# Loading and squaring q of two couples one couple sooner, w_in's loads on POOL's queue, and a one-column PSUM write on VectorE, in an attention and feed-forward kernel

## The chip, the cores and the metric

The kernel runs on one core of one Trainium2 chip. The metric is device time in microseconds, taken as the median of several runs. A core has five engines that are used here: PE (TensorE, the matrix engine, with its weight loads shown as PEld), DVE (VectorE), ACT (ScalarE), POOL (GpSimd) and SP (SyncE, which here only issues DMAs). Each engine works through its own queue in order, and engines wait for one another through semaphores.

## What is computed

The reference is an attention block with normalised queries and keys, followed by a feed-forward block:

```python
def rmsnorm(x, g):
    rms = np.sqrt(np.mean(x * x, axis=-1, keepdims=True) + 1e-06)
    return x / rms * g
q_n, k_n = rmsnorm(q, g_q), rmsnorm(k, g_k)
scores = matmul(q_n, k_n.T) / sqrt(head_dim)
attn = exp(scores - max); attn = attn / (sum(attn) + 1e-09)
x = matmul(attn, v)                     # then (B,H,S,D) -> (B*S, H*D)
h = x @ w_in
g = h * (1.0 / (1.0 + np.exp(-h)))
out = g @ w_out
```

q, k and v have the shape (8, 12, 448, 64): 8 batches, 12 heads, 448 positions, 64 values each. x has the shape (3584, 768), w_in (768, 2048), w_out (2048, 768). All data is float32 at the reference; w_in and w_out come to the kernel as 64-bit floats, read as words of 64 bits.

## The kernel before

The kernel works in two stages in one program. The first does attention and, woven into it, the first matrix product of the feed-forward block; its results go to a DRAM tensor `hidden`. The second stage, from about 760 us on, multiplies `hidden` by w_out. The change touches the first stage only.

The work of attention is cut into 24 couples, `c` = 0 to 23. A couple is four heads of one batch, so three couples make a batch. `GROUP` is 6 couples, two batches. Couples 0 to 5 (early) and 6 to 23 (late) are handled differently: an early couple's q and k are turned by PE (`transpose_q`, `transpose_k`), a late couple's by DVE's block transpose (`flip`). The late q is loaded as 32-row quarters (eight DMAs, `load_quarters`, L249).

For each couple the program emits `visit(c)` and then `between(c)`, and this emitted order is the order of each engine's queue: no scheduler moves anything.

`visit(c)` interleaves on PE the products of scores (`scores`, L701, followed by two exponentials on ACT, L706) with the products of weights and v (`weigh`, L738). The weighing accumulates into two PSUM banks from two row halves in turn. Between the two ways of placing halves, `turn` writes one column of the second bank (L714), so that PE's next weighing waits for the write, and the write for PE's last weighing. There are two such writes in a visit: `turn(1)` near its start, done by ACT in early visits and by DVE in late ones, and `turn(0)` past its middle, done by ACT in all visits before the change. Between them a late visit emits on DVE: `divide` (L796), then in visits 6, 12 and 18 `sum_x` (L825 and L828; twelve operations in visit 6, eight in the others), in visits 7 and 9 four sums of w_in (`sum_w_in`, L825), and in visits 8 and 10 two roundings of w_in (L122, L125, L129). After `turn(0)` the next work emitted on DVE is `add(c, 1)` (L752).

`between(c)` prepares the next couple. It emits `sum_up` (row sums of the exponentials on PE, L772), two reciprocals on DVE (L781), `spread` (six DMAs, L787 and L789), the turning of q and k, `gain` (L653, ACT, on the turned k) and the normalisation of a later couple: `sum_squares` (one ACT square, L661, and one DVE reduce, L662, of q), `normalise(...)[2:]` (two ACT squares, L458, two DVE reduces, L459, and L483 of k, followed by POOL's power, L487), and `scale` (a matmul with the identity, L673; L674 on DVE; power and product on POOL, L677 and L680). `pair_up` changes the identity once, with four POOL copies (L686), ahead of the first `scale`.

PE's time in `between` is filled by matmuls of the feed-forward product (L870). `fill(others, prompt)` takes steps from an iterator, as many as are due, and deals the pieces of `others` among them; the first piece of `prompt` is emitted at once, a further one after each third step, and the rest at the end. Between couples 3 and 5 little filler exists (`make_ahead`, twelve steps in five fills); from couple 6 on there is much more.

w_in is loaded in 24 pieces of 512 KB. A piece is loaded (L84), opened (two ACT operations, L99 and L100), rounded (three DVE operations and POOL's add, L133) and then used. `round` ends with up to two calls of `load`, each only if the buffer it fills has been rounded. Three loads stand in the prologue; the others are emitted by `round`, and SP issues all of them. The saves of the product to `hidden` are issued by SP too (L903), after the activation (L1008). They free one of three buffers of `stage`, into which ACT copies a product (L888).

Of the kernel before, what the change touches and what calls it, by code (L numbers as in the profile page):

```python
# [17 lines left out]
I64 = mybir.dt.int64  # L18
# [45 lines left out]
class Rounder:  # L64
# [3 lines left out]
    def __init__(self, nc, pieces):  # L68
        self.nc = nc
        self.pieces = pieces  # L70
        self.loaded = self.opened = self.rounded = 0

    def load(self):

        i = self.loaded
        if i == len(self.pieces):
            return False
        dst, src, raw, low = self.pieces[i]
        if raw[0] is not None and raw[0] >= self.rounded:
            return False  # L80
        self.loaded += 1
        raw = raw[1]
        if src.dtype == I64:
            self.nc.sync.dma_start(raw.bitcast(I64), src)  # L84
        return True

    def open(self):
# [439 lines left out]
def bounded(  # L527
# [13 lines left out]
    GROUP = z.NPAIR  # L541
# [27 lines left out]
    rows_q = [place["q0"], extra[:, 0:nq]]  # L569
# [6 lines left out]
    late = [extra[:, ds(2 * z.NW * S - (i + 1) * n, n)].bitcast(I32) for i in range(2)]  # L576
# [10 lines left out]
        return own["second_q"] if c == 1 else raw_q[c % 2]  # L587

    def q_of(c):
        return rows_q[c % 2 if c < GROUP else 0]  # L590

    def load_q(c):

        if 0 < c < NC:
            loads["q"](c, raw_of(c) if c < GROUP else q_of(c))
# [15 lines left out]
    def transpose_q(c):  # L611

        t = ps.tile([P, 2, BANK], F32, name="sc", bufs=2)
        both = [t[:, i] for i in range(2)]
        if c == 0:
            both[1] = ps.tile([P, BANK], F32, name="av1")
        for i in range(2):
            for j in range(J):
                rows = q_of(c)[0:R, ts(i * J + j, 2 * D)]
                nc.tensor.transpose(both[i][:, ts(j, R)], rows, ident[0:R, 0:R])  # L620
            if c == 0:
                (nc.scalar.copy, nc.vector.tensor_copy)[i](qT[:, i], both[i][:, 0:S])
        if c > 0:
            nc.scalar.copy(qT, t[:, :, 0:S])
        if c == GROUP - 2:
            load_q(GROUP)

    def transpose_k(c):

# [11 lines left out]
    def flip(c, name):  # L641

        if name == "q":
            nc.vector.transpose(qT.rearrange("p i s -> p (i s)"), q_of(c)[:, 0 : z.NK])
            load_q(c + 1)
            return
        nc.vector.transpose(kT, place["k1"])
        if c + 1 < NC:
            loads["quarters"](c + 1)
# [7 lines left out]
    def sum_squares(c):  # L657

        if c >= NC:
            return  # L660
        nc.scalar.activation(squares, q_of(c)[:, 0 : z.NK], AF.Square)  # L661
        nc.vector.tensor_reduce(  # L662
            out=norm.rms[c % 2][:, 0:n], in_=squares.rearrange("p (n e) -> p n e", e=z.Q),
            axis=AX.X, op=ALU.add,
        )
# [45 lines left out]
    def turn(step, copy):  # L711

        if step != weighed["step"]:
            copy(banks[1][:, S : S + 1], minus_half)  # L714
# [85 lines left out]
    def normalise(c):  # L800


        def piece(name, i):
            if name == "q":
                norm.squares_q(c, raw_of(c), scratch[i], i)
                norm.root(c, name, i)
                norm.scale(c, raw_of(c), q_of(c), i, nc.gpsimd)
                if i == 1 and c + 2 < GROUP:
                    load_q(c + 2)
            else:  # L810
                late = c >= GROUP
                rows = place["k0" if late else f"k{c % 2}"]
                norm.squares_k(c, rows, scratch[0 if late else i], i)
                if i == 1:
                    norm.root(c, name)
                    if late and c + 1 < NC:
                        loads["k"](c + 1)

        if c >= NC:
            return []  # L820
        return [lambda a=a: piece(*a) for a in (("q", 0), ("q", 1), ("k", 0), ("k", 1))]
# [540 lines left out]

    def visit(c):

        if c < GROUP - 1:
            beside = normalise(c + 1)
        elif c == GROUP - 1:
            beside = [lambda: sum_squares(c + 1), lambda: scale(c + 1)] + normalise(c + 1)[2:]
        else:
            beside = []  # L1370
        if c < NC:
            scores(c, 0, 0)
        run_all(beside[0:1])
        if c > 0:
            weigh(c - 1, LEFT)
            weigh(c - 1, LEFT - 1, 0)
            turn(1, nc.scalar.copy if c < GROUP else nc.vector.tensor_copy)
        if c < NC:
            scores(c, 0, 1)
        if c == 0:  # L1380
            run_all(beside[1:2])
        if c > 0:
            weigh(c - 1, LEFT - 1, 1)
            if c - 1 < EARLY:
                for i in range(2):
                    nc.vector.tensor_copy(x_of(c - 1, i), sums[i])
                run_all(beside[1:2])
                if inverting:
                    if c > 1:
                        divide(c - 2, None)  # L1390
                    run_all(inverting)
                    inverting.clear()
            else:
                divide(c - 1, sums)
                run_all(beside[1:2])
                if c < NC and c % GROUP == 0:
                    for i in range(0 if c == GROUP else 1, HW):
                        sum_x(last_two(c), i)
                weights_in_visit(c)
            if c + 1 < NC:  # L1400
                loads["vrest"](c + 1)
        if c == NC:
            return
        scores(c, 1, 0)
        scores(c, 1, 1)
        if c < GROUP:
            run_all(beside[2:3])
        weigh(c, 0, 1)
        scores(c, 2, 0)
        weigh(c, 1, 1)  # L1410
        turn(0, nc.scalar.copy)
        if c < GROUP:
            run_all(beside[3:4])
        scores(c, 2, 1)
        weigh(c, 0, 0)
        run_all(add(c, 1))
        weigh(c, 1, 0)
        scores(c, LEFT)
        if c + 1 < NC:
            loads["v"](c + 1)  # L1420

    def run_all(work):
        for piece in work:
            piece()

    def between(c):

        def transposes_and_sums():
            summing = sum_up(c)
            if c < GROUP:  # L1430
                next(summing)
            if c < GROUP - 1:
                transpose_k(c + 1)
            reciprocals = next(summing)
            if GROUP - 1 <= c < NC - 1:
                reciprocals += [lambda: flip(c + 1, "k"), gain]
            if GROUP // 2 <= c <= EARLY:
                divide(c - 1, None)
            return reciprocals

        if c < GROUP - 1:
            transpose_q(c + 1)
        elif c < NC - 1:
            flip(c + 1, "q")
        if c < GROUP // 2:
            inverting.extend(transposes_and_sums())
        elif c == GROUP - 1:
            run_all(transposes_and_sums())
        if c >= GROUP and c % GROUP == 0:
            fetched = range(AHEAD) if c == GROUP else ()  # L1450
            columns = products - 2 * HW * S * len(fetched)
            work = halves_in(last_two(c), range(HF), plain_in, dict(begun), fetched)
            begin(work, columns, 2 * GROUP)
            begun.clear()
        late = add(c, LEFT - 1) + add(c, LEFT) if c >= GROUP else []
        further = normalise(c + 2)[2:] if c >= GROUP - 1 else []
        queries = [lambda: sum_squares(c + 2)] if c >= GROUP - 1 else []
        fill(late + weights_in(c, 0) + further)
        prompt = transposes_and_sums() if GROUP // 2 <= c != GROUP - 1 else []
        if c == GROUP // 2:  # L1460
            begin(make_ahead([0, 1]), AHEAD * 2 * HW * S, GROUP - 1)
        fill(weights_in(c, 1), prompt[:3] + [lambda: run_all(prompt[3:] + queries)])
        if c == GROUP - 2:
            pair_up()
        if c % GROUP == GROUP - 1:
            finish()
            if c == GROUP - 1:
                begun[0] = fetch_ahead([0, 1], 0)
            else:
                sum_x([c // GROUP * 2, c // GROUP * 2 + 1], 0)  # L1470
        if c >= GROUP - 1:
            scale(c + 2)
        if GROUP <= c < NC - 1:

            nc.scalar.activation(first, minus_half, AF.Exp)
        if c == NC - 1:
            while rounder.load():
                pass
# [2 lines left out]
    load_q(2)  # L1481
    for _ in range(2):
        room.w_in.load()
    transpose_k(0)
    transpose_q(0)
    for c in range(NC):
# [228 lines left out]
```

## Time and profile before

| what | value |
|---|---|
| median of 3 runs | 1344.02 us (1342.76 to 1345.15) |
| the profiled execution, its own time | 1346.0 us |
| its span, first to last instruction | 1344.1 us |
| mean granted clock of TensorE | 0.994 |
| first column write of a late visit (L714 on DVE) | 19 instances, median 0.162 us |
| column writes on ACT (L714) | 29 instances, median 0.173 us |
| w_in loads issued by SP (L84) | 24 of 512 KB, some 5 us to landing |
| DMAs issued by POOL in the whole run | 4, of 0.539 to 0.759 us on POOL each |

The profile is one execution taken by the hardware profiler. A row of its timeline has the start in microseconds from the span's start, the length, the engine (a q behind it is the sequencer that issues a DMA), the line of the program, the operation, what is written and read, the shape and a count; in square brackets stands the idle time of the engine before it and what ended that. A matmul of float32 shows as two records. A table by windows gives for each stretch its length, the busy time of PE, PEld, DVE, ACT and POOL with counts, the granted clock, the DMA share and the rate. Holes of PE are read from the brackets in PE's rows.

### The profile page before, as it was taken

The page shows a single profiled execution, that of the slowest core. Times are in us where ns is not written, and L with a number is a line of the kernel's source. Part 1 is how long each engine was busy: PE and PEld are TensorE (multiplying, and loading weights), DVE is VectorE, ACT ScalarE, POOL GpSimd, SP SyncE. Part 2 cuts the span into 40 slices and gives each one's busy share as a digit, 9 for nine tenths or more (in the row PEclk, how much of TensorE's full clock was granted, in tenths as well). Part 3 has the DMA queues.
Part 4 walks back from the last instruction along what each step waited for, and adds up shares of the span by engine and source line. Part 5 has one row for each costly group of instructions (what it writes and reads, how often), then busy time and mean ns, then how long its engine had stood idle before and what let it go on. Part 6 is the DMA issues. An engine that isn't in the chain of part 4 may idle for free.

```text
span 1344.1 us, 19812 instructions
## 1 busy us (share of the span) xinstructions
PE 1300.4 (97%) x7111; PEld 828.3 (62%) x7111; DVE 951.8 (71%) x1630; ACT 502.3 (37%) x877; POOL 369.5 (27%) x223
## 2 busy tenths in 40 slices
PE   8997998999999999999999999999999999999997
PEld 4332443444444444444444455557999999999997
DVE  5786876785855655855554586789978787878785
ACT  7874455556445545455544244420000000101000
POOL 5765344443343343343331044410000000000000
PEclk9998999999999999999999999999999999999999
DMA  8565456434433543443421257422323232332311
GB/s 230 155 147 123 119 155 161 106 89 109 108 91 88 124 93 87 124 97 86 112 74 38 101 176 262 149 98 71 103 75 99 75 102 77 99 100 79 125 48 39
DMA packets 286543, 147.69 MB, mean 110 GB/s; under 512 B 224420, under 2 KB 270372, under 8 KB 286436
## 3 DMA queue, kind: packets, MB, share of 16 engines
q1 hardware_dynamic: 285872, 145.35, 39.6%
q8 instruction: 58, 0.95, 0.3%
q0 software_dynamic: 256, 0.79, 0.2%
q14 instruction: 49, 0.40, 0.1%
q10 hardware_dynamic: 308, 0.20, 0.0%
HBM read 96.73 MB, written 41.29 MB: 103 GB/s over the span
## 4 chain that ended last, share of the span: by engine, by line
PE 81%; DVE 7%; ACT 4%; DMA 3%; issue 2%; SPq 2%; POOL 0%; ACTq 0%; DVEq 0%
PE mm L870 24%; PE alone L1177 22%; PE av L738 8%; PE sc L701 8%; PE mm L1177 7%; PE alone L870 7%; PE alone L1214 2%; DVE work L781 1%; DVE work L752 1%; DMA rows<-in_k_dram 1%; PE sc L772 1%; SPq L249 1%; DVE sums_x L825 1%; PE mm L1214 1%; ACT L1008 1%
## 5 line engine op out<-in xcount | busy, mean ns | idle before, releaser
L870 PE MATMUL mm<-x,W 128*128 128x448 f32 x636 | 258.6, 549 | 12.0 <-DVE parts L828 3.3
L706 ACT ACTIVATE work<-sc,rms 128x448 f32<-128x448 f32 x324 | 185.5, 635 | 86.2 <-PE sc L701 62.8
L870 PEld LDWEIGHTS mm<-x,W 128*128 128x128 f32 x636 | 117.6, 191 | 146.8 <-issue 114.7
L870 PE MATMUL mm<-sums_x,W 128*128 128x448 f32 x456 | 186.5, 548 | 6.8 <-DVE parts L828 4.8
L701 PE MATMUL sc<-work 64*64 64x448 f32 x1344 | 167.3, 550 | 1.7 <-DVE rms L674 1.1
L738 PE MATMUL av<-work,rows 64*64 64x448 f32 x1296 | 156.0, 546 | 4.7 <-ACT av L714 1.8
L752 DVE TENSOR_TENSOR work<-work 128x896 f32<-128x896 f32 (+1 forms) x114 | 123.7, 1115 | 49.4 <-PE av L738 48.8
L870 PEld LDWEIGHTS mm<-sums_x,W 128*128 128x128 f32 x456 | 85.1, 191 | 100.2 <-issue 83.4
L487 POOL TENSOR_TENSOR rms<-rms,minus_half 128x14 f32<-128x14 f32 (+3 forms) x37 | 88.3, 2389 | 134.6 <-DVE rms L483 133.9
L514 POOL DMA_DIRECT2D out_dram<-x x2 | 1.3, 652 | 443.0 <-DVE x L828 443.0
L1177 PE MATMUL alone<-W,rows 128*128 128x192 f32 x608 | 113.0, 326 | 0.0
L738 PEld LDWEIGHTS av<-work,rows 64*64 64x64 f32 x1296 | 60.7, 133 | 76.0 <-issue 35.4
L677 POOL TENSOR_TENSOR rms<-rms,minus_half 128x28 f32<-128x28 f32 x18 | 86.2, 4791 | 74.7 <-DVE rms L674 63.3
L1177 PEld LDWEIGHTS alone<-W,rows 128*128 128x128 f32 x608 | 101.2, 190 | 0.0
L701 PEld LDWEIGHTS sc<-work 64*64 64x64 f32 x1344 | 55.5, 134 | 69.1 <-ACT work L706 26.9
L890 POOL TENSOR_TENSOR parts<-parts,stage 128x448 f32<-128x448 f32 x31 | 42.0, 1355 | 150.3 <-DVE parts L828 149.9
L1177 PE MATMUL alone<-W,work 128*128 128x192 f32 x382 | 72.2, 326 | 0.0
L1008 ACT ACTIVATE stage<-stage 128x896 f32<-128x896 f32 x63 | 57.4, 947 | 24.7 <-DVE stage L828 24.1
L1177 PEld LDWEIGHTS alone<-W,work 128*128 128x128 f32 x382 | 63.8, 190 | 0.0
L1187 ACT COPY rows<-alone 128x192 f32<-128x192 f32 x34 | 10.9, 320 | 137.4 <-PE alone L1177 78.9
L781 DVE RECIPROCAL work<-sc 128x224 f32<-128x224 f32 x36 | 55.6, 1547 | 5.2 <-PE sc L772 5.0
L459 DVE TENSOR_REDUCE rms<-rows 128x8 f32<-128x512 f32 (+2 forms) x48 | 30.2, 629 | 40.3 <-ACT rows L458 37.5
(243 smaller groups left out, 2104.9 us busy)
## 6 DMA issues: line engine op xcount, KB each, us to landing
hidden<-stage SPq DMA_DIRECT2D x63, 448.0 KB, 3.1
work<-hidden SPq DMA_DIRECT2D x21, 1024.0 KB, 5.1
rows<-in_moe_w_out_dram SPq DMA_DIRECT2D x32, 384.0 KB, 3.4
W<-in_moe_w_in_dram SPq DMA_DIRECT2D x22, 512.0 KB, 5.0
work<-work SPq DMA_DIRECT2D x144, 56.0 KB, 2.0
rows<-in_q_dram SPq DMA_DIRECT2D x144, 56.0 KB, 2.3
rows<-in_k_dram SPq DMA_DIRECT2D x144, 56.0 KB, 2.4
x<-hidden SPq DMA_DIRECT2D x7, 1024.0 KB, 5.6
```

The costliest lines, as they stand in the source:

```text
L487: nc.gpsimd.tensor_tensor(out=t, in0=t, in1=half, op=ALU.pow)
L677: nc.gpsimd.tensor_tensor(out=f, in0=f, in1=minus_half.to_broadcast([P, n]), op=ALU.pow)
L701: nc.tensor.matmul(two[ds(half * D, D), h, 0:S], keys[rows, ts(half, D)], qT[rows, pair, :], start=True, stop=True,)
L706: nc.scalar.activation(eleft[:, h] if j == LEFT else weights(c, j)[:, i, h], two[:, h, 0:S], AF.Exp, scale=norm.column(c, i, h, j),)
L738: nc.tensor.matmul(sums[i][ds(h * D, D), :], v, w, start=(j == 0 and step == 1), stop=(j == LEFT - 1 and step == 1),)
L752: nc.vector.tensor_tensor(out=total, in0=total, in1=more, op=ALU.add)
L781: nc.vector.reciprocal(out=r[0][:, rows], in_=t[:, rows])
L870: nc.tensor.matmul(t, self.left(name, s), self.right(name, s), start=s == ends[0], stop=s == ends[1])
L890: nc.gpsimd.tensor_tensor(out=u2, in0=u2, in1=p5, op=ALU.add)
L1008: nc.scalar.activation(t, t, AF.Silu)
L1177: nc.tensor.matmul(t, x[:, i], y, start=i == ORDER[0], stop=i == ORDER[-1])
L1214: nc.tensor.matmul(o, a[:, 2 * i + m, t], right_one(name, i)[:, m], start=n == 0, stop=n == len(steps) - 1,)
```

## The change

Four things are edited together.

The q of couple 6 is squared and scaled, and its k squared, in `between(4)` and no longer in `visit(5)`. The q of couple 7 is loaded by `transpose_q(5)` in `between(4)` (before: by `flip(6, "q")` in `between(5)`), into the buffer that q of couple 5 leaves; q of couple 8 is loaded by `flip(6, "q")`, and `flip(7, "q")` loads nothing.

In `between(5)`, `transposes_and_sums` is no longer run as a whole ahead of the first fill. Its PE part still is; the two reciprocals, the spreading, the flip of k and `gain` are handed to that fill as `prompt`.

The w_in loads that `round` emits are issued by POOL.

`turn(0)` of visits 6 to 23 is a DVE copy.

```diff
@@ class Rounder
+        self.queue = nc.sync
...
-            self.nc.sync.dma_start(raw.bitcast(I64), src)
+            self.queue.dma_start(raw.bitcast(I64), src)
@@ q_of(c)
-        return rows_q[c % 2 if c < GROUP else 0]
+        return rows_q[c % 2 if c < GROUP + 2 else 0]
@@ transpose_q(c)
-        if c == GROUP - 2:
-            load_q(GROUP)
+        if c >= GROUP - 2:
+            load_q(c + 2)
@@ flip(c, name)
-            load_q(c + 1)
+            if c != GROUP + 1:
+                load_q(c + 2 if c == GROUP else c + 1)
@@ visit(c)
-        if c < GROUP - 1:
-            beside = normalise(c + 1)
-        elif c == GROUP - 1:
-            beside = [lambda: sum_squares(c + 1), lambda: scale(c + 1)] + normalise(c + 1)[2:]
-        else:
-            beside = []
+        beside = normalise(c + 1) if c < GROUP - 1 else []
...
-        turn(0, nc.scalar.copy)
+        turn(0, nc.scalar.copy if c < GROUP else nc.vector.tensor_copy)
@@ between(c)
-        elif c == GROUP - 1:
-            run_all(transposes_and_sums())
...
-        further = normalise(c + 2)[2:] if c >= GROUP - 1 else []
-        queries = [lambda: sum_squares(c + 2)] if c >= GROUP - 1 else []
-        fill(late + weights_in(c, 0) + further)
+        further = normalise(c + 2)[2:] if c >= GROUP - 2 else []
+        queries = [lambda: sum_squares(c + 2)] if c >= GROUP - 2 else []
+        prompt = transposes_and_sums() if c == GROUP - 1 else []
+        fill(late + weights_in(c, 0) + further, prompt)
...
-        if c >= GROUP - 1:
+        if c >= GROUP - 2:
             scale(c + 2)
@@ bounded, ahead of the loop over couples
     for _ in range(2):
         room.w_in.load()
+    room.w_in.queue = nc.gpsimd
```

## The prediction

> **What bounds the kernel now.** I read the page first, then PE's row of the timeline for holes, then the engine named as the releaser of each hole, in the stretches that the change touches. The page says that PE is the bound:
>
> ```profile
> span 1344.1 us, 19812 instructions
> ...
> PE 1300.4 (97%) x7111; PEld 828.3 (62%) x7111; DVE 951.8 (71%) x1630; ACT 502.3 (37%) x877; POOL 369.5 (27%) x223
> ```
>
> So an edit counts only as far as it opens or shuts a hole in PE, and 97% is an average: the holes lie in a few places. Three of them bear on this change. The first is between couple 5 and couple 6 (PE's timeline):
>
> ```profile
> 119.36 1.02 PE L870 MATMUL mm<-x,W 128*128 128x448 f32 x2
> 122.76 4.12 PE L870 MATMUL mm<-x,W 128*128 128x448 f32 x6 [2.38 <-DVE work L781]
> 130.80 0.62 PE L673 MATMUL sc<-rms,ident 128*128 128x28 f32 x2 [3.92 <-DVE rms L662]
> 131.36 1.03 PE L701 MATMUL sc<-work 64*64 64x448 f32 x4
> ```
>
> PE waits 2.38 us for the reciprocal, then 3.92 us for the reduce of `sum_squares(7)`. Only four matmuls of filler (eight records) lie in this gap, so DVE and ACT set its length. Two stretches of the table by windows show a third loss, the clock, after the hole and its twin near 232 us:
>
> ```profile
> 129.47:132.88 3.41, 2.08 (x10) 1.05 (x14) 3.15 (x6) 1.26 (x3) 2.59 (x2) 0.50 0.59 102
> 132.88:136.29 3.41, 3.41 (x24) 1.24 (x20) 0.12 (x2) 1.16 (x2) 3.41 (x2) 0.50 0.61 118
> 235.28:238.69 3.41, 3.41 (x6) 1.38 (x6) 2.39 (x3) 0.60 (x1) 2.19 (x3) 0.50 0.17 43
> ```
>
> The value after POOL's is the granted clock, 0.50. A 3.41 us stretch in which PE stood idle for 2.02 us or more is followed by one at half clock, which costs 3.41/2 = 1.7 us of matmuls.
>
> The second place is the gap after couple 8 (timelines of SP, ACT and PE):
>
> ```profile
> 203.58 1.52 SPq L249 DMA_DIRECT2D rows<-in_k_dram  x3
> 213.00 3.51 SPq L84 DMA_DIRECT2D W<-in_moe_w_in_dram  x2
> ```
> ```profile
> 226.22 0.90 SPq L903 DMA_DIRECT2D hidden<-stage  x2
> ```
> ```profile
> 229.50 0.53 ACT L888 COPY stage<-mm 128x448 f32<-128x448 f32 x1 [8.56 <-DMA hidden<-stage]
> ```
> ```profile
> 230.08 2.52 PE L870 MATMUL mm<-x,W 128*128 128x448 f32 x6 [2.55 <-ACT stage L888]
> 234.62 2.00 PE L870 MATMUL mm<-sums_x,W 128*128 128x448 f32 x3 [2.02 <-DVE parts L828]
> ```
>
> SP stands from 205.1 to 213.0 behind a w_in load that waits for POOL's add. So the saves of hidden issue at 226.2, ACT waits 8.56 us for the first to land, and PE waits 2.55 and 2.02 us and then runs one stretch at half clock.
>
> The third place is visit(6), in DVE's timeline and in the one of the moment when the one-column write runs on ACT:
>
> ```profile
> 137.90 1.16 DVE L796 TENSOR_TENSOR x<-av,work 128x448 f32<-128x448 f32 x2 [1.55 <-PE av L738]
> 138.97 1.73 DVE L825 TENSOR_TENSOR sums_x<-x 128x448 f32<-128x448 f32 x1
> ...
> 146.34 0.62 DVE L825 TENSOR_TENSOR sums_x<-x,sums_x 128x448 f32<-128x448 f32 x1
> 146.87 1.08 DVE L752 TENSOR_TENSOR work<-work 128x896 f32<-128x896 f32 x1
> ```
> ```profile
> 141.96 0.17 ACT L714 COPY av<-minus_half 128x1 f32<-128x1 f32 x1
> 142.19 0.14 PEld L738 LDWEIGHTS av<-work,rows 64*64 64x64 f32 x3 [0.35 <-ACT av L714]
> ```
>
> PE's next weighing is released by the write at 142.13, while DVE works through twelve `sum_x` operations without a pause until 146.96. L752 at 146.87 is `add(6, 1)`, the first DVE instruction that stands after the write in the emitted order.
>
> [...]drops at 2.02 us of idle within a window, but not at 1.6 us (the hole before 151.5 us). [...]the four POOL issues of this trace take 0.54 to 0.76 us each. [...](an L825 of 0.62 us takes 2.12 us beside POOL L680 at 353.95).
>
> **The write on VectorE.** `turn(0)` of couples 6 to 23 moves into DVE's in-order queue, behind `divide`, `sum_x` and `weights_in_visit`. Where DVE is idle (11 visits; DVE idles 4.44 us before L752 in visit 11) nothing is lost; PE's start follows ACT's copy by 0.05 us, so at most 11 x 0.05 = 0.5 us is gained. In seven visits DVE is behind. The write then starts where L752 starts now, takes 0.16 us (DVE's L714 median), and PE follows 0.05 us later. L752's start plus 0.21, less PE's present start: visit 6: 147.08-142.19 = 4.9; visit 7: 179.29-177.26 = 2.0; visit 8: 214.12-211.76 = 2.4; visit 9: 253.74-251.80 = 1.9; visit 10: 287.65-285.29 = 2.4; visit 12: 357.92-354.99 = 2.9; visit 18: 562.26-559.25 = 3.0. Sum 19.5 us. Queued behind the write on DVE is only `add(c, 1)`, which waits for that weighing and so starts some 1.3 us later. PE arrives later at holes that DVE sets now, which gives back: after visit 6 holes of 1.97 and 0.49; after visit 7 about 0.7 (what 2.0 exceeds DVE's 1.3); after 8 about 0.5 of 1.03; after 9 0.3; after 10 about 1.2 of 1.86 and 0.94. Together 5.2, leaving 14.3. After visits 12 and 18 no such hole follows, so their 5.9 us stay whole. Idle stretches of 2 to 5 us also trip the clock: bounds 0 and 7 x 1.7 = 12 us. [...]I take about half, 5.5.
>
> **Couple 6 squared in the gap before visit 5.** `normalise(6)` for k (two ACT squares, two DVE reduces, L483), `sum_squares(6)` and `scale(6)` leave visit(5), where PE hid them but for a hole of 0.24 and two matmuls (0.55 in all). They enter between(4), where the filler is short. DVE's rows there:
>
> ```profile
> 103.04 0.95 DVE L825 TENSOR_TENSOR W<-W 128x768 f32<-128x768 f32 x1
> 103.90 1.55 DVE L781 RECIPROCAL work<-mm 128x224 f32<-128x224 f32 x1
> 106.59 1.09 DVE L662 TENSOR_REDUCE rms<-rows 128x28 f32<-128x896 f32 x1 [1.14 <-ACT av L714]
> ```
>
> DVE ends this work at 105.45 while PE enters visit(5) at 103.36. The added reduces, 0.69+0.55+0.18 with their ping-pong with ACT, push `divide(3)` from 98.02 to 99.7, and the second reciprocal to about 106.8; L662 (1.09), now queued behind it, ends at 107.9, and the matmul of `scale(6)` stands ahead of visit(5) on PE. PE starts visit(5) at 108.25: +4.9, less 0.55. POOL's four copies of `pair_up` end near 107.3, just before. The hole of 3.4 us or so trips the clock: +1.7 (bounds 0 and 3.4).
>
> **Couple 7, one gap later.** q(7)'s eight loads now issue in between(4), but their landing (125.5) was not what L662 waited for: ACT's third square started at 128.68, on the reduce before it. The number of DVE and ACT operations in between(5) is unchanged; `run_all` becomes pieces dealt in the fill, so squares and rounding stand ahead of the second reciprocal, flip and `gain`. Counting from the end of visit(5)'s matmuls (115.64 before): adds +1.0, flip 2.1, divide 3.2, reciprocal 4.75, rounding 6.35, two reduces and L483 8.4, reciprocal 9.95, flip 11.0, `gain` 12.05, square 13.0, reduce 14.1; before, the matmul of `scale(7)` came at +15.16. So 1.0 is saved, and the slow clock ends about 1.1 us cheaper, because more of it falls into the hole. The loads of q(7), k(7), q(8) and k(8) that pass the spreading DMAs on SP delay these by some 4 us; `divide(4)` and `divide(5)` come later still, so this is hidden. This part: 4.35+1.7-1.0-1.1 = +4.0.
>
> **Loads on POOL.** 21 of the 24 w_in loads leave SP. Elsewhere SP's wait for POOL, or the 0.4 us of each issue, ended in no hole of PE. After couple 8 it did: saves would issue near 223, land near 226, and PE would not wait: -2.55-2.02-1.7 = -6.3 (bounds: 0, if the late q loads or the stage buffers hold the saves, and -6.3). POOL pays about 0.65 us for each[...]. Most lie in idle POOL; the four after couple 0 push q of couple 2 from 38.0 to 39.4, and PE wants it at 39.3. I take +0.7 in all[...].
>
> **The sum.** 14.3 + 5.5 - 0.5 + 4.0 - 6.3 + 0.7 = +17.7. Against the profiled execution that is 1346.0 (span 1344.1, 1.9 around it) to 1363.7; the median shown, 1344.0, lies 2.0 below that execution, so the forecast is 1361.7.
>
> **Rivals.** *Given back*: the DVE-bound stretches after visits 6 to 10 return all but 2.4 of those five waits and the clock never drops: 5.9+2.4-0.5+2.3-6.3+0.7 = +4.5, 1348.5. For it: five holes set by DVE follow there. Against: the clock did drop after 2.02 us.[...] *The other side*: in between(5) the reordering lets filler and reduces run beside each other, so both holes and the slow clock shut: 2.38+3.92 and about 4.2 of clock = -10.5; with -6.3 after couple 8 and waits of 14.3 without clock loss: -10.5-6.3+14.3-0.5+0.7 = -2.3, 1341.7. It decides once the waits net under some 16 us. Against: the same chain of DVE and ACT operations remains and there is no more filler. That the write isn't held by DVE's queue I exclude: L752 shows that queue in order.
>
> **Chances.** Forecast 0.73 (1351 to 1373 by its bounds), given back 0.12[...], the other side 0.07. Range 1348 to 1373: it takes in the lower rival and leaves out the other side[...]. About 0.2% (2.7 us) can be told from no change: faster 0.07, same 0.04, slower 0.89.
>
> **What would show it.** DVE L714 with 37 instances; PE holes before L738 released by DVE L714 of 2 to 5 us in visits 6 to 10, 12 and 18; a hole of 3 to 4 us before L673 ahead of visit(5); no ACT wait of 8 us for hidden<-stage after couple 8. I am wrong if those PE holes are under 1 us, or if between(5) shrinks by more than 3 us.

## The result, and the profile after

| | median, us | runs |
|---|---|---|
| before | 1343.65 (1342.76 to 1345.15) | 4 |
| after | 1363.36 (1362.46 to 1364.35) | 4 |

The ratio is 1.0146, 95% interval 1.0128 to 1.0163: slower by 19.7 us. The forecast was 1361.7. The profiled execution of after has a span of 1362.5 us (its own time 1364.35), 18.4 more than the one of before. In after the lines of the code named here stand one or two further down: the column write is L716, the weighing L740, the filler L872, the matmul of `scale` L675, the reduce of `sum_squares` L664. The page of after:

```profile
span 1362.5 us, 19838 instructions
...
PE 1305.3 (96%) x7111; PEld 826.0 (61%) x7111; DVE 951.5 (70%) x1648; ACT 500.7 (37%) x859; POOL 379.2 (28%) x244
...
L740 PE MATMUL av<-work,rows 64*64 64x448 f32 x1296 | 161.0, 564 | 21.8 <-DVE av L716 16.5
```

PE has the same 7111 records and 4.9 us more of busy time: matmuls at half clock, which are longer (below, 3.26 us for sixteen records where 1.73 is seen at full clock). The other 13.5 of the 18.4 us are idle time of PE. DVE and ACT swap eighteen instructions and POOL gains its 21 issues, and none of these engines is busier in a way that matters. The last line says where: of 21.8 us that PE stood idle ahead of the weighing, 16.5 were ended by DVE's write. The table of PE's waits in after (line that waited, releaser, us in total, times, longest) sets this beside the others:

```profile
PE av L740 <- DVE av L716: 16.5, 7, 4.3
PE sc L675 <- DVE rms L664: 10.6, 3, 6.8
PE mm L872 <- DVE parts L830: 3.7, 6, 1.7
PE av L740 <- DMA rows<-in_v_dram: 2.5, 1, 2.5
```

In the kernel before the same table has 1.5 us (once, in the last visit) in place of the 16.5, 4.7 in place of the 10.6, 8.1 in place of the 3.7 for the row of parts, and 0.9 in place of the 2.5 for v: each of the changed parts shows in this table.

**The write.** The timeline of PE in after, in visits 6, 9, 12 and 18:

```profile
145.94 1.20 PE L703 MATMUL sc<-work 64*64 64x448 f32 x8
151.40 3.26 PE L740 MATMUL av<-work,rows 64*64 64x448 f32 x16 [4.25 <-DVE av L716]
...
258.27 1.73 PE L740 MATMUL av<-work,rows 64*64 64x448 f32 x16
...
365.13 2.21 PE L740 MATMUL av<-work,rows 64*64 64x448 f32 x16 [2.56 <-DVE av L716]
...
573.84 2.70 PE L740 MATMUL av<-work,rows 64*64 64x448 f32 x16 [2.58 <-DVE av L716]
```

The other holes of this kind are 1.62 us (visit 7, at 187.05), 1.93 (visit 8, at 223.70) and 2.01 (visit 10, at 293.67). In visit 9 there is none to speak of: 0.14 us. DVE's timeline shows why PE waits in visit 6; the one-column write comes directly behind the last of twelve sums, without a pause:

```profile
150.66 0.62 DVE L827 TENSOR_TENSOR sums_x<-x,sums_x 128x448 f32<-128x448 f32 x1
151.19 0.15 DVE L716 COPY av<-minus_half 128x1 f32<-128x1 f32 x1
```

And the table by windows (length; busy us of PE, PEld, DVE, ACT, POOL; granted clock; DMA share; GB/s) shows what follows such a hole. The stretch after it runs at half clock, and the 3.26 us of the sixteen records at 151.40 compare with 1.73 for sixteen at 258.27:

```profile
147.78:151.20 3.42, 0.00 (x0) 0.00 (x0) 3.39 (x8) 0.58 (x2) 0.00 (x0) 1.00 0.05 10
151.20:154.61 3.41, 3.21 (x20) 1.21 (x24) 1.45 (x4) 0.00 (x0) 0.00 (x0) 0.50 0.00 0
```

(Matmuls begun before 147.78 end there by the model, so PE's 0.00 in the first row is the hole.)

**The gaps before visits 5 and 6.** PE and then DVE in after:

```profile
103.91 1.77 PE L872 MATMUL mm<-x,W 128*128 128x448 f32 x4 [2.23 <-DVE stage L830]
108.80 0.38 PE L675 MATMUL sc<-rms,ident 128*128 128x28 f32 x2 [3.12 <-DVE rms L664]
...
135.24 0.60 PE L675 MATMUL sc<-rms,ident 128*128 128x28 f32 x2 [6.77 <-DVE rms L664]
```
```profile
106.16 1.55 DVE L783 RECIPROCAL work<-mm 128x224 f32<-128x224 f32 x1
107.63 1.03 DVE L664 TENSOR_REDUCE rms<-rows 128x28 f32<-128x896 f32 x1
```

Before visit 5 the reduce now stands behind the second reciprocal and ends at 108.66, and PE waits for it. Before visit 6 the two holes of 2.38 and 3.92 us have become one of 6.77.

**After couple 8.** SP, ACT and PE in after:

```profile
228.00 5.40 SPq L250 DMA_DIRECT2D rows<-in_q_dram  x8
233.50 0.90 SPq L905 DMA_DIRECT2D hidden<-stage  x2
```
```profile
236.85 0.53 ACT L890 COPY stage<-mm 128x448 f32<-128x448 f32 x1 [4.15 <-DMA hidden<-stage]
```
```profile
236.98 3.27 PE L872 MATMUL mm<-x,W 128*128 128x448 f32 x8
241.97 2.52 PE L872 MATMUL mm<-sums_x,W 128*128 128x448 f32 x6 [1.72 <-DVE parts L830]
```

ACT still waits for the saves, now behind the eight loads of q and not behind w_in, but for 4.15 us in place of 8.56. The hole of 2.55 us is gone, that of 2.02 is 1.72, and no half-clock stretch follows. This can't be put down to the loads on POOL alone: e2 and e9 below shorten the same gap with all loads on SP.

**What no case of the prediction had: v of visit 2.** PE, POOL and SP in after:

```profile
51.09 0.98 PE L740 MATMUL av<-work,rows 64*64 64x448 f32 x8 [2.46 <-DMA rows<-in_v_dram]
```
```profile
42.73 1.17 POOL L85 DMA_DIRECT2D W<-in_moe_w_in_dram  x2
46.68 0.55 POOL L85 DMA_DIRECT2D W<-in_moe_w_in_dram  x1 [0.30 <-POOL W L134]
```
```profile
43.52 0.53 SPq L321 DMA_DIRECT2D rows<-in_v_dram  x1
44.10 1.68 SPq L324 DMA_DIRECT2D rows<-in_v_dram  x2
```

The first of these three loads of v lands 6.4 us after its issue (in before, where it is issued at 43.72, 3.4 us), with three pieces of w_in of 512 KB each on the way at the same time (e5 shows that these are the cause). In before, SP issued them at 49.70, behind v and k in its queue. The hole is followed by a half-clock stretch from 52.2.

The ledger of the two profiled executions, by the starts and ends of the scores of each visit:

| part | predicted, us | after less before, us |
|---|---|---|
| visits 6, 7, 8, 9, 10, 12, 18 (waits and clock) | 19.5 + 5.5 | 6.2 + 1.9 + 2.2 + 0.4 + 3.7 + 4.4 + 4.5 = 23.3 |
| gaps behind 6, 7, 9 and 10 | -4.7 | -2.8 (6), -0.2 (9), -2.5 (10) = -5.5 |
| gap before visit 5, and visit 5 | +4.35 + 1.7 | 4.5 + 0.5 = 5.0 |
| gap before visit 6 | -1.0 - 1.1 | -1.8 |
| gap after couple 8 (the write, the loads on POOL) | -0.5 - 6.3 | -5.9 |
| visits 2 to 4 (POOL's price) | +0.7 | 3.9 - 1.3 = 2.6 |
| idle visits | -0.5 | within the remainder |
| start, before visit 1 | 0 | -1.3 |
| behind visit 23 | 0 | +2.3 |

The right column sums to 18.7, the spans differ by 18.4. (The 4.4 of visit 12 has 0.4 of the gap behind it.) The -1.3 at the start is there with only the write moved too (-1.4), where nothing in that place was touched; it is scatter between executions.

### The profile page after: what moved, and what is told of

Same layout as the page of the kernel before. It is cut to its first block, busy times and chain, and to the rows that moved or that the text cites. A ratio compares the mean times of both kernels' runs of the same rounds, so it can differ in the third digit from the quotient of the medians.

```text
span 1362.5 us, 19838 instructions
## 1 busy us (share of the span) xinstructions
PE 1305.3 (96%) x7111; PEld 826.0 (61%) x7111; DVE 951.5 (70%) x1648; ACT 500.7 (37%) x859; POOL 379.2 (28%) x244
## 4 chain that ended last, share of the span: by engine, by line
PE 78%; DVE 11%; DMA 3%; ACT 3%; SPq 2%; issue 2%; POOL 0%; ACTq 0%; DVEq 0%; POOLq 0%
PE mm L872 22%; PE alone L1179 22%; PE av L740 8%; PE mm L1179 7%; PE alone L872 7%; PE sc L703 7%; PE alone L1216 2%; SPq L250 2%; DVE sums_x L827 2%; DVE work L783 1%; DMA rows<-in_k_dram 1%; PE sc L774 1%; DVE W L827 1%; DVE work L754 1%; DMA work<-work 1%
## 5 line engine op out<-in xcount | busy, mean ns | idle before, releaser
L872 PE MATMUL mm<-x,W 128*128 128x448 f32 x636 | 256.8, 547 | 6.1 <-DVE stage L830 3.1
L872 PEld LDWEIGHTS mm<-x,W 128*128 128x128 f32 x636 | 117.2, 190 | 140.4 <-issue 112.2
L872 PE MATMUL mm<-sums_x,W 128*128 128x448 f32 x456 | 184.7, 544 | 3.1 <-DVE parts L830 2.3
L740 PE MATMUL av<-work,rows 64*64 64x448 f32 x1296 | 161.0, 564 | 21.8 <-DVE av L716 16.5
L703 PE MATMUL sc<-work 64*64 64x448 f32 x1344 | 170.1, 559 | 2.2 <-DVE rms L676 1.2
L872 PEld LDWEIGHTS mm<-sums_x,W 128*128 128x128 f32 x456 | 85.1, 190 | 95.6 <-issue 85.5
L754 DVE TENSOR_TENSOR work<-work 128x896 f32<-128x896 f32 (+1 forms) x114 | 121.8, 1099 | 25.9 <-PE av L740 24.2
L740 PEld LDWEIGHTS av<-work,rows 64*64 64x64 f32 x1296 | 59.3, 136 | 98.9 <-issue 38.9
L1189 ACT COPY rows<-alone 128x192 f32<-128x192 f32 x34 | 10.8, 318 | 136.9 <-PE alone L1179 88.2
L1193 ACT COPY rows<-alone 128x192 f32<-128x192 f32 x34 | 10.8, 319 | 123.7 <-PE alone L1179 120.1
```

The costliest lines, as they stand in the source:

```text
L703: nc.tensor.matmul(two[ds(half * D, D), h, 0:S], keys[rows, ts(half, D)], qT[rows, pair, :], start=True, stop=True,)
L740: nc.tensor.matmul(sums[i][ds(h * D, D), :], v, w, start=(j == 0 and step == 1), stop=(j == LEFT - 1 and step == 1),)
L754: nc.vector.tensor_tensor(out=total, in0=total, in1=more, op=ALU.add)
L872: nc.tensor.matmul(t, self.left(name, s), self.right(name, s), start=s == ends[0], stop=s == ends[1])
```

## The experiments

All these kernels compute everything that the reference asks for. Times are medians; each ratio is to runs of the kernel before on the same chip.

**e1: all of the change but the write.** After, with

```diff
-        turn(0, nc.scalar.copy if c < GROUP else nc.vector.tensor_copy)
+        turn(0, nc.scalar.copy)
```

> The changed kernel with turn(0) of the late visits back on ACT, all else as changed. Theory (the write queued behind DVE's work in seven visits is the main cost, some 18 to 20 us with the clock it trips): 1343 to 1346 us; no hole of PE before the weighing of visits 6 to 10, 12 and 18 over 0.3 us, granted clock 1.0 from visit 8 to the end of the stage but for chance. Rival (the early squaring of couple 6 is the main cost, the write's waits are mostly given back): at least 1355 us.

Measured: 1346.53 us, ratio 1.0028 (1.0017 to 1.0038). That is half a microsecond above what was expected. By the medians the write is worth 16.8 us of the 19.7. Of the holes that DVE's write sets before a weighing, only the one of 1.5 us in the last visit is left, and before has that too.

**e2: the write alone.** Before, with the line of e1 the other way round.

> The kernel before with turn(0) of visits 6 to 23 on DVE alone. Theory: slower than before by 14 to 20 us (1358 to 1364), with holes released by DVE's write of about 4.9, 2.0, 2.4, 1.9, 2.4, 2.9 and 3.0 us less what PE's skew hides, in visits 6 to 10, 12 and 18, and none over 0.2 us in the other eleven. Rival: slower by under 8 us, since the holes set by DVE after visits 6 to 10 shrink by as much.

Measured: 1363.79 us, ratio 1.0153 (1.0139 to 1.0167), inside the expected 1358 to 1364. The holes, in PE's timeline of this kernel:

```profile
143.88 3.26 PE L738 MATMUL av<-work,rows 64*64 64x448 f32 x16 [4.87 <-DVE av L714]
...
256.38 1.73 PE L738 MATMUL av<-work,rows 64*64 64x448 f32 x16 [1.53 <-DVE av L714]
```

The first is as long as the 4.9 us that were worked out for visit 6, and visit 9 has its hole here. So the 0.14 us of visit 9 in after belongs to the other parts: there DVE gets to its write 8.7 us after the start of the visit, here after 10.1. The loads on POOL have a share in that: with them alone DVE gets to `add` in visit 9 after 9.65 us (e3 and e5), in before after 10.10. The rest isn't settled.

By the starts and ends of the scores, the seven visits are 26.5 us longer than in before, and the gaps behind visits 6 to 10 are 3.0, 0.0, 3.9, 0.4 and 2.5 us shorter, 9.7 in all. (This trace lies 1.6 us below the median of its kernel and that of before 2.1 above its own, so the spans differ by 16.3 us where the medians differ by 19.9.) After couple 8 the hole of 2.55 us is gone here too, though SP issues all loads: PE comes later.

**e3: w_in's loads on POOL alone.** Before, with

```diff
+        self.queue = nc.sync
...
-            self.nc.sync.dma_start(raw.bitcast(I64), src)
+            self.queue.dma_start(raw.bitcast(I64), src)
...
+    room.w_in.queue = nc.gpsimd
```

> The kernel before with the w_in loads that round emits issued by POOL, alone. Theory: faster than before by 4 to 6 us (1338 to 1340): the 8.6 us wait of ACT for hidden<-stage after couple 8, PE's holes of 2.55 and 2.02 us and the half clock there are gone (-6.3), and a hole of some 2 us in visit 2, where v lands late, costs 1 to 2. Rival (issues on POOL are dear for POOL and DVE): no faster than before, 1343 us or more.

Measured: 1343.88 us, ratio 1.0000 (0.9992 to 1.0008). A miss: the gap after couple 8 is 4.9 us shorter, but there is a loss around visit 2. Its hole in PE's timeline of this kernel, in which the lines stand one further down than before:

```profile
51.39 1.77 PE L739 MATMUL av<-work,rows 64*64 64x448 f32 x8 [2.68 <-DMA rows<-in_v_dram]
```

With the half-clock stretch behind it, visit 2 is 3.8 us longer; from the end of visit 1 to the end of visit 4 the loss is 2.7. Of the 4.9 us after couple 8, 2.0 show also where nothing in that place was touched (see e9), which leaves 2.9 for the loads: gain and loss about cancel.

**e5: the same loads on POOL, but only from couple 6 on.** Made after e3, to see whether the hole comes from those early issues. As e3, with the last line put inside the loop over couples, under `if c == GROUP:`.

> The kernel before with the w_in loads issued by POOL only from couple 6 on, by SP until then. Theory (issuing on POOL gains some 5 us after couple 8 and loses it in visits 1 to 4, where w_in's packets run beside those of v and k instead of behind them): the hole of 2.7 us in visit 2 is gone, the one after couple 8 stays gone, 1338 to 1340.5 us. Rival (POOL's own time for the issues is the loss, wherever they are): 1342 us or more.

Measured: 1340.88 us, ratio 0.9980 (0.9971 to 0.9988): faster than before by 2.5 us, and just above what was expected. Two views of this kernel, SP and PE:

```profile
224.08 0.90 SPq L904 DMA_DIRECT2D hidden<-stage  x2
```
```profile
47.90 1.68 PE L702 MATMUL sc<-work 64*64 64x448 f32 x16
49.57 0.98 PE L739 MATMUL av<-work,rows 64*64 64x448 f32 x8
...
232.08 2.52 PE L871 MATMUL mm<-sums_x,W 128*128 128x448 f32 x6 [1.49 <-DVE parts L829]
```

The weighing at 49.57 follows without a hole, and the saves, issued at 224.08 and not at 226.22, leave only the hole of 1.49 us behind couple 8 (that gap is 4.8 us shorter, with the same 2.0 in it). The early issues on POOL are thus what costs in visit 2; by the medians of e3 and e5 they cost 2.5 us.

**e4: the early squaring and the dealing, without the write and without POOL.** After, with the write as in e1 and without the line `room.w_in.queue = nc.gpsimd`.

> The changed kernel without the write on DVE and without the loads on POOL: only the earlier q and k of couples 6 to 8 and the pieces dealt in the gap after couple 5. Theory: slower than before by 2.5 to 5 us (1346.5 to 1349): PE waits some 3 us for DVE's reduce ahead of visit 5, then runs one stretch at half clock, and the gap after couple 5 is 1 to 2 us shorter. Rival (the early loads and squares do what they are for, and the trace of the changed kernel shows the loads on POOL in their way): faster than before by 2 us or more.

Measured: 1345.74 us, ratio 1.0020 (1.0013 to 1.0026): slower, but at 1.8 us by the medians short of the 2.5 to 5 that were expected. PE's timeline of this kernel:

```profile
102.43 3.20 PE L872 MATMUL mm<-x,W 128*128 128x448 f32 x4 [2.24 <-DVE stage L830]
107.32 0.38 PE L675 MATMUL sc<-rms,ident 128*128 128x28 f32 x2 [1.69 <-DVE rms L664]
```

Visit 5 starts 4.3 us later, near the 4.9 that was foreseen, and takes 11.12 us in place of 12.35, since the norms of couple 6 have left it. The half clock lies from 102.6 to 106.0, over the four records of filler (3.20 us, in after 1.77) whose end PE's wait follows anyway; so it costs nothing. In after it lies over visit 5, which takes 12.81 us.

**e7: the dealing alone**, with q(7) and q(8) loaded sooner and couple 6 still squared in visit 5. Before, with the change's edits of `q_of`, `transpose_q` and `flip`, and with

```diff
-        elif c == GROUP - 1:
-            run_all(transposes_and_sums())
...
-        fill(late + weights_in(c, 0) + further)
+        prompt = transposes_and_sums() if c == GROUP - 1 else []
+        fill(late + weights_in(c, 0) + further, prompt)
```

> The kernel before with the gap after couple 5 dealt as in the change (reciprocals, flip and gain as prompt pieces of the fill; q of couples 7 and 8 loaded one couple sooner), but couple 6 squared and scaled in visit 5 as before. Theory (the gap after couple 5 gains 1 to 2 us, and the early squaring ahead of visit 5 is what loses): faster than before by 1 to 3 us (1341 to 1343). Rival (the dealing is what loses): slower than before.

Measured: 1344.53 us, ratio 1.0006 (0.9997 to 1.0015): no difference to be told, and a miss. PE before visit 6, in this kernel:

```profile
122.16 2.52 PE L872 MATMUL mm<-x,W 128*128 128x448 f32 x6 [0.62 <-ACT stage L880]
131.45 0.60 PE L675 MATMUL sc<-rms,ident 128*128 128x28 f32 x2 [6.77 <-DVE rms L664]
```

The hole of 2.38 us moved into the one of 3.92; the gap is 0.5 us shorter (15.14 for 15.65), not 2. In e4 and in after it is 1.8 shorter. DVE's timeline shows why, in e7 and then in e4:

```profile
115.36 1.45 DVE L484 TENSOR_SCALAR rms<-rms 128x14 f32<-128x14 f32 x1
116.73 2.09 DVE L754 TENSOR_TENSOR x<-x,work 128x896 f32<-128x896 f32 x2
```
```profile
117.35 2.09 DVE L754 TENSOR_TENSOR x<-x,work 128x896 f32<-128x896 f32 x2 [4.48 <-PE av L740]
```

L754 opens DVE's work for this gap, and from its start to the matmul of `scale` it is 14.7 us in both (15.2 in before). In e7 it stands behind the last piece of couple 6's normalisation and starts together with PE's row sums (116.77); in e4 DVE has been idle for 4.48 us, and it starts 1.3 us ahead of them (118.67). So the dealing is worth 0.5 us, and the other 1.3 come from the norms that have left visit 5.

**e8: e7 and e5 together.**

> The dealing of the gap after couple 5 and the loads on POOL from couple 6 on, together; turn(0) on ACT, couple 6 squared in visit 5. Theory: the two gains lie in different gaps and add up, 1335 to 1338.5 us, faster than both kernels. Rival: the first gain is eaten by a later wait, and it is as the run with the late loads on POOL alone.

Measured: 1339.94 us, ratio 0.9972 (0.9961 to 0.9983): above what was expected by about as much as e7 was, and at 3.5 us under the kernel before the fastest of all kernels here; its interval overlaps that of e5, so what the dealing adds isn't shown.

**e6: the write on DVE, put ahead of DVE's sums.** Before, with

```diff
-        if c > EARLY:
-            if c < NC and c % GROUP == 0:
-                for i in range(0 if c == GROUP else 1, HW):
-                    sum_x(last_two(c), i)
-            weights_in_visit(c)
...
-        turn(0, nc.scalar.copy)
+        turn(0, nc.scalar.copy if c < GROUP else nc.vector.tensor_copy)
+        if c > EARLY:
+            if c < NC and c % GROUP == 0:
+                for i in range(0 if c == GROUP else 1, HW):
+                    sum_x(last_two(c), i)
+            weights_in_visit(c)
```

> The kernel before with turn(0) of late visits on DVE, and sum_x and the rounding and summing of w_in in visits emitted just behind that write instead of ahead of it. Theory (the place in DVE's queue is the cost, not the engine): no hole before the weighing over 0.3 us in visits 6 to 10, 12 and 18, and a time within 5 us of the kernel before (1342 to 1349), as add(c, 1) now comes later. Rival (a DVE write of PSUM releases PE later than an ACT write, or collides with other DVE work): holes of over 1 us stay and the time is over 1352.

Measured: 1355.57 us, ratio 1.0076 (1.0062 to 1.0090). Half a hit: the holes before the weighing are gone, so it was the place in the queue; but the time lies where the rival had it. DVE and PE in this kernel:

```profile
140.49 0.16 DVE L714 COPY av<-minus_half 128x1 f32<-128x1 f32 x1 [2.83 <-PE av L738]
140.56 0.62 DVE L825 TENSOR_TENSOR sums_x<-x 128x448 f32<-128x448 f32 x1
```
```profile
146.42 1.77 PE L870 MATMUL mm<-sums_x,W 128*128 128x448 f32 x4 [1.24 <-DVE sums_x L825]
...
157.31 1.02 PE L870 MATMUL mm<-sums_x,W 128*128 128x448 f32 x2 [2.22 <-DVE parts L828]
```

Now DVE stands idle for 2.83 us until PE's weighing lets it write, its sums begin that much later, and PE waits for the sums: the gaps behind visits 6, 7, 9, 10, 12 and 18 are 13.1 us longer together. Here the write costs on both sides: what is ahead of it delays it (e2), and what is behind it is delayed by what the write waits for (e6).

**e9, e10, e11: the write on DVE in some visits only.** Before, with `nc.vector.tensor_copy` in `turn(0)` for visits 12 and 18 (e9), for the eleven visits in which DVE is idle (e10), and for visits 6 to 10 (e11).

> The kernel before, with the second one-column write on VectorE in visits 12 and 18 only. Theory (the write waits in VectorE's queue, and nothing that follows these two visits gives the wait back): two PE holes of 2.5 to 3 us before the weighing, 5.9 us in all, each with one half-clock stretch of 1.7 us: 5.9 to 9.3 us over the kernel before, 1349.5 to 1353. Rival (PE's later arrival is absorbed by the next thing that VectorE or ScalarE would have held up, as after visits 6 to 10): under 1346.

> The kernel before, with that write on VectorE in visits 11, 13 to 17 and 19 to 23 only, where VectorE has nothing queued ahead of it. Theory (only the place in the queue costs, VectorE itself is not dearer than ScalarE for one column): within 1 us of the kernel before, 1342.7 to 1344.5, with no PE hole over 1 us before these weighings. Rival (the write on VectorE costs by itself in each of the eighteen visits, some 1.1 us each): about 1356.

> The kernel before, with that write on VectorE in visits 6 to 10 only. Theory (waits of some 13 us in all, of which about 5 are given back at holes that VectorE sets already, and a few half-clock stretches): what the write costs alone (about 20 us) less what visits 12 and 18 cost, so 10 to 14 us over the kernel before, 1353.5 to 1358. Rival (nearly all is given back after these visits): under 1348.

Measured: e9 1355.47 us, ratio 1.0088 (1.0074 to 1.0101); e10 1343.86, ratio 1.0002 (0.9994 to 1.0010); e11 1349.83, ratio 1.0052 (1.0039 to 1.0066). Above the kernel before, by medians, 12.3, 0.7 and 6.7 us, together 19.7, where e2 has 19.9. So the eleven writes are free, and only the place in the queue costs. But by these medians two visits out of seven make most of the price: e9 came out 2.5 us above the theory's range, e11 3.7 us below it. PE's timeline and the table by windows of e9:

```profile
356.73 2.50 PE L738 MATMUL av<-work,rows 64*64 64x448 f32 x16 [2.56 <-DVE av L714]
...
565.42 2.97 PE L738 MATMUL av<-work,rows 64*64 64x448 f32 x16 [2.58 <-DVE av L714]
```
```profile
354.35:357.76 3.41, 1.03 (x12) 0.59 (x16) 2.29 (x5) 1.03 (x2) 0.04 (x1) 0.97 0.00 0
357.76:361.18 3.42, 3.42 (x17) 0.96 (x11) 2.42 (x3) 0.38 (x1) 0.00 (x0) 0.53 0.15 35
```

In this execution (its own time is 1354.3) visit 12 is 4.3 and visit 18 is 4.5 us longer: 8.8 together, 5.9 of wait and some 3 of clock, as the theory has it, and they keep it to the end. The profiled execution of before (1346.0) is 8.3 below that. But it lies 2.9 above the median of the seventeen runs of before here, and the one of e9 1.1 below its own; so about 4 us of the 12.3 are in no trace. Where they are stays open. Differences between executions do show in places that no edit touches; in e9 the largest is the gap after couple 8, 2.0 us shorter than in before. PE's timeline of e9 there:

```profile
230.24 3.87 PE L870 MATMUL mm<-x,W 128*128 128x448 f32 x6 [2.00 <-ACT stage L888]
234.78 2.52 PE L870 MATMUL mm<-sums_x,W 128*128 128x448 f32 x6 [0.67 <-DVE parts L828]
```

Here the half-clock stretch (from 231.27) lies over the six records between the two holes, 3.87 us for 2.52 in before, and fills most of the second, 0.67 us in place of 2.02; in before it came behind both (from 235.28) and cost its full 1.7. In e10 the longest waits for the same two releasers, ACT's copy and DVE's parts, are 2.3 and 2.1 us, near the two holes of before.

What e11 has too little is in its trace: visits 6 to 10 are 15.8 us longer and the gaps behind them 9.1 shorter, not 5, which makes the 6.7 that were measured.

## Why the prediction was right, point by point

**The time.** 1361.7 was forecast and 1363.36 measured. The main term was right; that the sum came so near is partly luck. By themselves the parts measure +19.9 (the write, e2; 19.3 predicted), +1.8 (couple 6 and the dealing, e4; +4.0) and -0.1 (the loads, e3; -6.3 + 0.7 = -5.6): two errors in opposite directions, -2.2 and +5.5. The three add up to 21.6 and the change measures 19.7; the intervals of the change and of e2, about 2 us either way, don't tell the two sums apart.

**The write on VectorE: right in mechanism and, as a sum, in size.** Its terms were 14.3 + 5.5 - 0.5 = 19.3 us; alone it measures 19.9 (e2), with the others in place 16.8 (after less e1). The rule used, that PE starts where L752 started plus 0.21 us, is borne out: against the start of its visit PE's weighing comes later in e2 than in before by 2.03, 2.36, 1.93, 2.35, 2.94 and 3.01 us in visits 7 to 10, 12 and 18, each within 0.01 us of the rule. (The holes are some 0.4 us shorter than these delays.) In visit 6 it is 4.2 in e2 and 4.8 in after, for 4.9; why it is less in e2 was not shown. Visit 9's 1.9 was mis-sized for after, where the hole is 0.14. What is given back was put at 5.2; the gaps of e2 return 9.7 and those of e11 9.1, of which 2.0 after couple 8 needn't be the write's (e9). In e2 the visits are longer than worked out too, 26.5 for 25.0. That visits 12 and 18 keep theirs was right, and e9 shows it. The 0.5 us gained in idle visits isn't there: in visit 11 PE's weighing does start 0.05 us sooner, but the visit is no shorter (e10).

**The clock: right in kind and nearly in size.** 5.5 us were put on the seven waits. In the profile of after the stretches behind visits 6, 10, 12 and 18 drop, those behind 7, 8 and 9 don't: four times 1.3 to 1.5 us beyond the delay itself, 5.7 together. (Granted clock 0.50 from 151.2, 294.6, 366.3 and 574.5, after holes of 4.25, 2.01, 2.56 and 2.58 us; 1.00 after those of 1.62, 1.93 and 0.14.) What wasn't counted is that the clock also changes at holes that were harmless. Behind visit 23 after loses another 2.3 us in a place that no edit touches. The table by windows, after and then before:

```profile
772.50:775.90 3.40, 0.98 (x8) 0.21 (x8) 2.30 (x7) 0.00 (x0) 0.00 (x0) 0.99 0.80 239
775.90:779.30 3.40, 3.18 (x5) 1.57 (x6) 3.33 (x7) 0.00 (x0) 0.00 (x0) 0.50 0.62 243
```
```profile
754.09:757.50 3.41, 2.09 (x18) 0.51 (x16) 2.76 (x5) 0.95 (x1) 0.00 (x0) 1.00 0.43 176
757.50:760.91 3.41, 1.83 (x11) 0.71 (x12) 2.27 (x6) 0.00 (x0) 0.00 (x0) 1.00 0.98 315
```

Both kernels have the same two holes there, 1.54 and 1.37 us (1.53 and 1.37 before). In after they fall into one stretch (3.40 less 0.98 is 2.42 us idle), in before the border at 757.50 cuts them into 1.32 and 1.58, and nothing happens. This is the place of the borders, not PE's delay: e3, at the end of visit 23 3.1 us ahead of before, loses 2.8 us there.

**Couple 6 squared sooner: right in after, too large alone.** The reduce behind the second reciprocal was put at 107.9; in after it ends at 108.66, with visit 4 ending 1.3 us later than in before. The gap before visit 5 grows by 4.5 us there and in e4, for 4.9. The 0.55 us that visit 5 was to lose are 1.2 (e4). The 1.7 of clock is there in after (12.81 less 11.12) and costs nothing in e4. With the gap before visit 6, the part was to cost +4.0: in after it is 5.0 - 1.8 = 3.2, in e4 +1.8.

**The dealing: the number was right, the reason only in part.** -1.0 and -1.1 of clock were put on it, and the gap shrank by 1.8 in after and in e4. But 0.5 of that is the dealing's (e7), and 1.3 come from DVE being free earlier, an effect of the edit to couple 6 that was not counted. What the slow clock saves shows in visit 6, not in this gap, and is 0.4 us in e4, not 1.1. That the two numbers met is luck.

**The loads on POOL: the step that failed.** The prediction wrote "POOL pays about 0.65 us for each" and took "+0.7 in all", against a gain of 6.3 after couple 8. The issues do take 0.53 to 0.75 us. But the price isn't POOL's time. Where the early loads land wasn't looked up: in visit 2 they run beside v, which visit 2 needs at once. That makes visit 2 3.9 us longer in after and 3.8 in e3; with what the next visits and gaps return, the loss is 2.6 and 2.7. The gain was over-sized as well. The -5.9 of after doesn't confirm the -6.3: the write alone shortens that gap by 3.9 (e2), and 2.0 of it come and go between executions (e9). By medians the loads gain 2.5 us where only the late ones are moved (e5) and nothing where all are (e3). The traces show as much: three loads of v that took 2.6 to 3.4 us to landing in before take 5.1 to 6.4 in after, beside w_in, and in e5, in which SP issues w_in behind them, the weighing at 49.57 follows without a hole. How the transfers share the DMA engines was not shown.

**The rivals.** "Given back" fell: it had the gaps return all but 2.4 us of the five waits and no half clock, and visits 6 to 10 alone cost 6.7 (e11). That POOL's own time for the issues is the loss (the rival of e5) fell: each takes 0.53 to 0.75 us in after, and e5 is 2.5 us faster than before. The other side needed both holes before visit 6 to shut, and they became one of 6.77.

**The signs.** DVE's 37 column writes, the hole of 3 to 4 us ahead of visit 5 (3.12) and the end of ACT's wait of 8 us came as named. Of the seven holes of 2 to 5 us, four lie in that range, two are 1.6 and 1.9, and visit 9's is 0.14.

## What to carry to other kernels

A tiny instruction costs what its place in an in-order queue costs: here a write of some 0.16 us cost 19.9 us in eighteen visits (e2), and 0.7 us, within the interval of no change, in the eleven in which DVE is idle (e10). Look up where the next instruction behind the new place starts today: that is when it will run; and what it must wait for is then paid by all that is queued behind it, so moving it forward (e6) can trade one hole for another. A load moved to another queue loses its order behind the loads that it used to follow (in visit 2 w_in, which SP issued at 49.70 behind v and k, is issued by POOL from 42.73 on, and the first v lands after 6.4 us in place of 3.4); ask which transfer will be in the air beside it, and move only those that end a stall (e5: faster by 2.5 us; all of them, e3: nothing).

## What the runs showed of the hardware that was not expected

- Where the borders of the 3.41 us stretches fall decided what the two holes behind visit 23 cost: within one stretch (after, 2.42 us idle) they brought half clock and a loss of 2.3 us, cut into 1.32 and 1.58 us by a border (before) they brought none. The 2.55 us hole after couple 8 in before has a border in it too, at 228.45, which leaves 1.63 us idle in the stretch behind it, and the clock is 1.00 in the next. The borders differ from one execution to another: 9.5 us after the start of the span the same four matmul records (L620 into av, in after L621) take 1.01 us in before and 0.60 in after. So single profiles of two kernels can differ by some us in untouched places, as by the 2.3 here.
- Idle time of two holes counted together: 1.54 and 1.37 us in one stretch (2.42 us idle) brought half clock. In the clock records of before and after, from 20 us on, every stretch at full clock with 1.96 us or more of idle PE is followed by half clock, and none with 1.86 us or less. That is what these two executions show; no run looked for a limit.
- What a half-clock stretch costs depends on what lies under it. The one after couple 8 cost 1.7 us in before, behind both holes, and little in e9, where it filled the second hole (0.67 us left of 2.02). With it over four records of filler ahead of a wait (e4: 3.20 us for 1.77) it cost nothing.
- Two holes of 2.6 us (e9) lengthened their visits by 8.8 us, and nothing gave that back. Five of 1.5 to 4.5 us (e11) lengthened theirs by 15.8 us and cost 6.7: the length of a hole alone didn't tell its price.
- Three pieces of 512 KB on another queue nearly doubled the time to landing of small loads (v: 3.4 to 6.4 us).
